# Second expert's rows asked for in front of weights, y's main part scaled first, and an early register load

## The chip, the cores and the metric

The kernel runs on one core of a Trainium2 chip. The metric is the device time of one execution in microseconds. The engines that the text names: PE is TensorE's matmul side and PEld its weight loads, DVE is VectorE, ACT is ScalarE, POOL is GpSimd, SP is SyncE, whose queue issues nearly all plain transfers. A name with a q behind it (PEq, POOLq) is the engine's sequencer.

## The reference

Sliding-window attention feeds a gated product layer, and its result goes to a mixture of eight experts with one expert per token. The last part is the one that matters here:

```python
logits = x @ w_gate
expert_idx = np.argmax(logits, axis=1)
...
gate_w = probs[np.arange(N), expert_idx]
...            # disp[e, pos] = x[i], at most `capacity` rows for each expert
h = np.maximum(np.einsum('ecd,edf->ecf', disp, w1), 0.0)
y = np.einsum('ecf,efd->ecd', h, w2)
for i in range(N):
    if keep[i]:
        out[i] = gate_w[i] * y[expert_idx[i], pos[i]]
```

There are 1152 tokens, 8 experts, d_model 512 and d_ff 1024, all in float32.

## The kernel before

Attention and the gated product layer come first. Each 128 of the resulting rows are then scattered by their expert to a table in DRAM, `disp`, with the gate weight and the token's number in two extra columns (`scatter`, L522). The largest count of tokens of any expert goes to `mxi` (L805), and 36 matmuls without use (`warm1`) follow on PE.

The expert stage goes over the experts e = 0 to 8 and over eight steps f of each (`layer1(e, f)` and, one expert behind, `layer2(e - 1, f)`). The code writes the order of the work on every engine by hand, so each engine's queue runs in the order in which the calls stand.

- `load_rows(ep, e)` (L547) reads the first 192 rows of expert e from `disp` into the tile `xr`, in two transfers of 128 and 64 rows on SP's queue.
- `x_tr(e)` (L558) transposes them on PE into two PSUM tiles `xt`; ACT (L71) and DVE (L72) split each into a high and a low part, `xs`. For expert e + 1 this is called at f = 5 of expert e.
- `layer1` (L575, L576) is four pairs of matmuls over `xs` and the weights `he`, `le`; `relu` (L583 ACT, L584 DVE, L586 ACT, L587 DVE, L590 POOL) makes `hs` of it.
- `layer2` (L604, L605 for the 64 tail rows; L607 to L609 for the 128 main rows) gathers the expert's result over its eight steps in two PSUM tiles of tag `y`, of which there are three banks. The main tile of each expert takes the bank that the main tile of the expert before had.
- `conv_e` splits the next piece of expert weights `st_e` into `he` (ACT, L71) and `le` (DVE, L72), and asks for a further piece on SP's queue (L113). With expert 0 it is called at f = 3 and f = 5 only, later at every f. The pieces have eight buffers in all, and SP waits at a piece whose buffer is not free yet, with all that is behind it in its queue.
- `y_tail` (L618 ACT, L619 DVE) scales the tail by the gate weight; `y_main` (L623 ACT) scales the main part; `y_out` (L627 POOL) scatters each to the output.

With expert 0, layer2 has no work yet, so a step is layer1 alone. Behind the expert stage the count in `mxi` is loaded to a register of each engine (L845), and a branch skips a part that is needed only if an expert has over 192 tokens.

Of the kernel before, what the change touches and what calls it, by code (L numbers as in the profile page):

```python
# [8 lines left out]
F32 = mybir.dt.float32  # L9
# [5 lines left out]
AF = mybir.ActivationFunctionType  # L15
# [3 lines left out]
P = 128  # L19
# [9 lines left out]
def block_kernel(ctx: ExitStack, tc: tile.TileContext, qT, kT, v, w1, w2, w3T, wo, wg, e1, e2, out):  # L29
    nc = tc.nc  # L30
    B, H, D, S = qT.shape
    DM = H * D
    NT = B * S
    DF = wo.shape[0] * P
    E = wg.shape[1]
# [22 lines left out]
    def slot(name, shape, dtype=F32R):  # L58
        t = big.tile([P, SLOT], dtype, tag="u", name=name)
        n = 1  # L60
        for d in shape:
            n *= d
        if len(shape) == 1:
            return t[:, :n]
        return t[:, :n].rearrange("p (a b) -> p a b", b=shape[1])
# [4 lines left out]
    def split(t, hi, lo, eng):  # L70
        nc.scalar.copy(out=hi, in_=t)  # L71
        eng.tensor_tensor(out=lo, in0=t, in1=hi.bitcast(F32), op=ALU.subtract)  # L72
# [469 lines left out]
    xr = {}  # L542

    def load_rows(ep, e):
        x = ep.tile([P, 2, RW], F32, tag="xr", name=f"xr{e}", bufs=4)
        for i, r, n in rows:
            nc.sync.dma_start(out=x[:n, i, :], in_=disp[e * CAP + r : e * CAP + r + n, :])  # L547
        xr[e] = x
# [3 lines left out]
    def x_tr(e):  # L552
        x = xr[e]
        tvs = [banks.tile([P, 512], F32, tag="t", name=f"xt{e}_{half}", bufs=2)[:, : 2 * N0].rearrange("p (a s) -> p a s", a=2) for half in range(2)]

        for i, r, n in rows:
            for dt in range(KD):
                nc.tensor.transpose(tvs[dt // 2][:, dt % 2, r : r + n], x[:n, i, dt * P : (dt + 1) * P], ident[:n, :n])  # L558
        for half, tv in enumerate(tvs):
            xt = slot(f"xs{e}_{half}", (2, 2 * N0))  # L560
            split(tv, xt[:, :, :N0], xt[:, :, N0:], nc.vector)
            xt_[e, 2 * half], xt_[e, 2 * half + 1] = xt[:, 0, :], xt[:, 1, :]
# [3 lines left out]
    def layer1(e, f):  # L566
        if f % 2 == 0:
            hs_[e, f // 2] = slot(f"hs{e}_{f // 2}", (2, 2 * N0 + NB))

        hp_ = banks.tile([P, 512], F32, tag="y" if e == 0 and f % 2 else "h", name=f"h{e}_{f}")  # L570
        hi, lo = (w.rearrange("p (k f) -> p k f", k=KD) for w in es[e, 0, f // 2])
        fs = slice(f % 2 * P, f % 2 * P + P)
        for kt in range(KD):
            xs = xt_[e, kt]
            nc.tensor.matmul(hp_[:, : 2 * N0], hi[:, kt, fs], xs, start=(kt == 0), stop=False)  # L575
            nc.tensor.matmul(hp_[:, N0 : 2 * N0], lo[:, kt, fs], xs[:, :N0], start=False, stop=(kt == KD - 1))  # L576
        live["h", e, f] = hp_

    def relu(ep, e, f, between=lambda: None):
        hp_ = live.pop(("h", e, f))  # L580
        h = hs_[e, f // 2][:, f % 2, :]
        cr = ep.tile([P, N0], F32, tag="cr", name=f"cr{e}_{f}", bufs=3)
        nc.scalar.copy(out=cr, in_=hp_[:, N0 : 2 * N0])  # L583
        nc.vector.tensor_tensor(out=hp_[:, :N0], in0=hp_[:, :N0], in1=cr, op=ALU.add)  # L584
        between()
        nc.scalar.activation(out=h[:, :N0], in_=hp_[:, :N0], func=AF.Relu)  # L586
        nc.vector.scalar_tensor_tensor(out=h[:, N0 : 2 * N0], in0=hp_[:, :N0], scalar=0.0, in1=h[:, :N0].bitcast(F32),  # L587
                                       op0=ALU.max, op1=ALU.subtract)

        nc.gpsimd.tensor_copy(h[:, 2 * N0 :], h[:, P:N0])  # L590

    yp_ = {}

    def layer2(e, kt, parts=(1, 0)):
        hi, lo = (w[:, kt % 2 * DM : kt % 2 * DM + DM] for w in es[e, 1, kt // 2])
        h = hs_[e, kt // 2][:, kt % 2, :]
        first, last = kt == 0, kt == EF // P - 1
        for tail in parts:
            if first:
                yp_[e, tail] = banks.tile([P, DM], F32, tag="y", name=f"y{tail}_{e}")  # L600
            yp = yp_[e, tail]
            if tail:
                ht = h[:, N0 + P :]
                nc.tensor.matmul(yp, ht, hi, start=first, stop=False)  # L604
                nc.tensor.matmul(yp, ht, lo, start=False, stop=last)  # L605
            else:
                nc.tensor.matmul(yp, h[:, :P], hi, start=first, stop=False)  # L607
                nc.tensor.matmul(yp, h[:, :P], lo, start=False, stop=False)  # L608
                nc.tensor.matmul(yp, h[:, N0 : N0 + P], hi, start=False, stop=last)  # L609

    ys_ = {}

    def y_tail(ep, e):
        w = xr[e][:NB, 1, DM : DM + 1]
        yb = yp_.pop((e, 1))
        y = ep.tile([P, 2, DM], F32, tag="y", name=f"y{e}")
        ys = ep.tile([P, DM], F32, tag="ys", name=f"ys{e}")
        nc.scalar.activation(out=ys[:NB], in_=yb[NB : 2 * NB], func=AF.Copy, scale=w)  # L618
        nc.vector.scalar_tensor_tensor(out=y[:NB, 1, :], in0=yb[:NB], scalar=w, in1=ys[:NB], op0=ALU.mult, op1=ALU.add)  # L619
        ys_[e] = y  # L620

    def y_main(e):
        nc.scalar.activation(out=ys_[e][:, 0, :], in_=yp_.pop((e, 0)), func=AF.Copy, scale=xr[e][:, 0, DM : DM + 1])  # L623

    def y_out(e, i):
        _, r, n = rows[i]
        put = nc.gpsimd.indirect_dma_start(  # L627
            out=out, out_offset=bass.IndirectOffsetOnAxis(ap=xr[e][:n, i, DM + 1 : DM + 2].bitcast(U32), axis=0),
            in_=ys_[e][:n, i, :], in_offset=None, bounds_check=NT - 1, oob_is_err=False)

        tc.declare_no_dep(put.ins, group="y_out", reason="rows of different tokens")
        tc.add_to_no_dep_group("y_out", put.ins)
# [129 lines left out]
    for i, u in enumerate(ab1):  # L762
# [3 lines left out]
        if i == 2:  # L766
            nc.sync.dma_start(out=disp[0 : E * CAP, :].rearrange("(p r) c -> p r c", p=P),
                              in_=zrow.unsqueeze(1).to_broadcast([P, E * CAP // P, RW]))
    for at in sorted(jobs):
        for job in jobs[at]:  # L770
            job()
    nc.sync.dma_start(out=out.rearrange("(p r) c -> p r c", p=P),
                      in_=zrow[:, :DM].unsqueeze(1).to_broadcast([P, NT // P, DM]))
# [29 lines left out]
    mxi = const.tile([P, 1], I32, name="mxi")  # L803
# [3 lines left out]
    cv_.close()  # L807
    front.close()


    ep = work.enter_context(tc.tile_pool(name="exp", bufs=2))
    banks = work.enter_context(tc.tile_pool(name="banks", bufs=3, space=bass.MemoryType.PSUM))
    deeper.append(ep)
    load_rows(ep, 0)
    x_tr(0)
    for _ in range(STAGES):
        stage_next()
    NF = EF // P
    for e in range(E + 1):
        for f in range(NF):  # L820
            if e < E:
                layer1(e, f)
                relu(ep, e, f, conv_e if e or f in (3, 5) else lambda: None)
                if f == 1 and e + 1 < E:
                    load_rows(ep, e + 1)
            if 0 < e < E:
                layer2(e - 1, f)
            if f == NF - 3 and e + 1 < E:
                x_tr(e + 1)
        if e == E:  # L830
            for part in (1, 0):
                for f in range(NF):
                    layer2(e - 1, f, (part,))
                if part:
                    y_tail(ep, e - 1)
                    y_out(e - 1, 1)
        elif e:
            y_tail(ep, e - 1)
            y_out(e - 1, 1)
        if e:  # L840
            y_main(e - 1)
            y_out(e - 1, 0)
    work.close()

    fullest = nc.values_load(mxi[0:1, 0:1], min_val=0, max_val=NT)  # L845
    with (tc.If(fullest > N0), tc.tile_pool(name="over", bufs=2) as op,
          tc.tile_pool(name="overp", bufs=2, space=bass.MemoryType.PSUM) as opp):
        for e in range(E):
# [6 lines left out]
            for r in range(N0, CAP, P):  # L855
# [16 lines left out]
                for f in range(EF // P):  # L872
                    nc.tensor.matmul(yp[:n], ht[:, f, :n], w2s[:, f, :], start=(f == 0), stop=(f == EF // P - 1))
                y = op.tile([P, DM], F32, tag="y", name=f"oy{e}_{r}")
                nc.vector.tensor_scalar_mul(y[:n], yp[:n], x[:n, DM : DM + 1])
                nc.gpsimd.indirect_dma_start(
                    out=out, out_offset=bass.IndirectOffsetOnAxis(ap=x[:n, DM + 1 : DM + 2].bitcast(U32), axis=0),
                    in_=y[:n], in_offset=None, bounds_check=NT - 1, oob_is_err=False)
# [45 lines left out]
```

## Time and profile before

| What | us |
|---|---|
| median of 3 runs | 486.1 (484.58 to 486.83) |
| the profiled execution, its own time | 483.7 |
| its span, from the first to the last instruction | 482.0 |
| PE busy | 458.3 |
| DVE busy | 322.7 |
| ACT busy | 261.6 |
| POOL busy | 143.0 |

The profiled execution lasts 1.7 us longer than its span. Busy times of an engine that others wait for say little on their own; where PE is not busy, the question is which wait ended last there.

### The profile page before, as it was taken

The numbers are of one execution on the slowest core, as the hardware profiler recorded it, in microseconds if no ns is written. First come the engines' busy times: TensorE is split into PE (matmuls) and PEld (weight loads), VectorE is DVE, ScalarE is ACT, GpSimd is POOL, SyncE is SP. The second block draws the span as 40 slices with busy tenths as digits, with TensorE's granted clock in tenths as the row PEclk, the third lists the DMA queues.
The fourth block names the chain that finished last, engine by engine and source line by source line (L and its number), as shares of the span: only waits on it lengthen the run. The fifth ranks groups of instructions, "written<-read, shape, count | busy, mean of one in ns | idle before, by whom it ended". The sixth has DMA issues, their size and how long they took to land.

```text
span 482.0 us, 9290 instructions
## 1 busy us (share of the span) xinstructions
PE 458.3 (95%) x3344; PEld 406.4 (84%) x3351; DVE 322.7 (67%) x863; ACT 261.6 (54%) x653; POOL 143.0 (30%) x151
## 2 busy tenths in 40 slices
PE   7999899999999999999999999949999999999993
PEld 3667587888999999999999998649898888888882
DVE  5788789688341645978847775246878777787740
ACT  4676667567231455344435552236767677676750
POOL 2113132213010232443402212013455454554531
PEclk9999899999999999999999999979999999999998
DMA  8655453222097233864504443354786887868001
GB/s 288 181 170 187 132 175 118 88 89 86 3 296 187 88 131 114 299 204 153 173 1 133 132 131 110 121 207 136 247 280 192 288 246 233 270 196 285 29 1 52
DMA packets 30769, 77.77 MB, mean 161 GB/s; under 512 B 3582, under 2 KB 9214, under 8 KB 30720
## 3 DMA queue, kind: packets, MB, share of 16 engines
q1 hardware_dynamic: 28976, 72.41, 48.3%
q0 software_dynamic: 1744, 4.73, 2.6%
q8 instruction: 28, 0.46, 0.4%
q14 instruction: 21, 0.17, 0.1%
HBM read 65.30 MB, written 12.61 MB: 162 GB/s over the span
## 4 chain that ended last, share of the span: by engine, by line
PE 74%; DVE 13%; ACT 4%; issue 4%; DMA 3%; SPq 1%; POOL 1%; POOLq 0%; DVEq 0%; ACTq 0%
PE h L575 10%; PE ab L373 7%; PE ab L375 6%; PE ab L374 6%; PE h L576 4%; PE x L469 4%; PE x L470 4%; PE x L471 4%; DVE t_w L140 4%; PE s L232 3%; PE t L300 3%; PE y L607 3%; PE warm L81 3%; PE oa L320 2%; PE y L608 2%
## 5 line engine op out<-in xcount | busy, mean ns | idle before, releaser
L72 DVE TENSOR_TENSOR le<-st_e,he 128x1024 fp32r<-128x1024 f32 x64 | 78.4, 1226 | 32.6 <-ACT he L71 25.9
L590 POOL CAST hs<-hs 128x64 fp32r<-128x64 f32 x64 | 56.1, 878 | 87.8 <-ACT hs L586 86.5
L575 PE MATMUL h<-xs,he 128*128 128x384 f32 x256 | 78.5, 364 | 1.1 <-DVE xs L72 1.1
L373 PE MATMUL ab<-x,wh 128*128 128x288 f32 x256 | 79.4, 310 | 0.0
L374 PE MATMUL ab<-x,wh 128*128 128x288 f32 x256 | 75.4, 295 | 0.0
L375 PE MATMUL ab<-x,wl 128*128 128x288 f32 x256 | 75.4, 294 | 0.0
L71 ACT CAST he<-st_e 128x1024 fp32r<-128x1024 f32 x64 | 67.3, 1052 | 0.0
L576 PE MATMUL h<-xs,le 128*128 128x192 f32 x256 | 64.9, 254 | 0.0
L575 PEld LDWEIGHTS h<-xs,he 128*128 128x128 f32 x256 | 49.1, 192 | 3.9 <-DVE xs L72 1.2
L373 PEld LDWEIGHTS ab<-x,wh 128*128 128x128 f32 x256 | 48.1, 188 | 4.9 <-issue 2.2
L576 PEld LDWEIGHTS h<-xs,le 128*128 128x128 f32 x256 | 49.7, 194 | 1.9
L374 PEld LDWEIGHTS ab<-x,wh 128*128 128x128 f32 x256 | 48.1, 188 | 0.0
L375 PEld LDWEIGHTS ab<-x,wl 128*128 128x128 f32 x256 | 48.0, 188 | 0.0
L383 DVE TENSOR_TENSOR g<-ab,asb 128x288 f32<-128x288 f32 x32 | 14.5, 455 | 46.1 <-PE ab L375 44.8
L258 ACT ACTIVATE p<-p,stat 128x256 f32<-128x256 f32 (+2 forms) x80 | 37.3, 470 | 13.1 <-DVE stat L247 13.0
L583 ACT COPY cr<-h 128x192 f32<-128x192 f32 x64 | 20.4, 318 | 43.4 <-PE h L576 41.4
L469 PE MATMUL x<-wph,gh 128*128 128x260 f32 x144 | 41.4, 287 | 0.0
L470 PE MATMUL x<-wpl,gh 128*128 128x260 f32 x144 | 40.6, 282 | 0.0
L471 PE MATMUL x<-wph,gl 128*128 128x260 f32 x144 | 40.6, 282 | 0.0
L378 ACT COPY asb<-ab 128x288 f32<-128x288 f32 x32 | 12.7, 397 | 47.7 <-PE ab L375 47.7
L435 PE MATMUL wp<-woh,w3h 128*128 128x260 f32 x128 | 36.3, 283 | 0.4 <-DVE wpl L72 0.4
L437 PE MATMUL wp<-woh,w3l 128*128 128x260 f32 x128 | 36.2, 283 | 0.0
(138 smaller groups left out, 1078.4 us busy)
## 6 DMA issues: line engine op xcount, KB each, us to landing
st_e<-e SPq DMA_DIRECT2D x64, 512.0 KB, 4.3
st_w<-w SPq DMA_DIRECT2D x16, 512.0 KB, 4.4
st_w<-w3T SPq DMA_DIRECT2D x16, 512.0 KB, 3.9
disp<-zrow SPq DMA_DIRECT2D x1, 4626.0 KB, 21.4
st_wo<-wo SPq DMA_DIRECT2D x8, 512.0 KB, 3.6
qk<-qT SPq DMA_DIRECT2D x8, 288.0 KB, 4.9
qk<-kT SPq DMA_DIRECT2D x8, 288.0 KB, 5.2
y<-zrow SPq DMA_DIRECT2D x1, 2304.0 KB, 10.9
```

The source lines that it names most:

```text
L71: nc.scalar.copy(out=hi, in_=t)
L72: eng.tensor_tensor(out=lo, in0=t, in1=hi.bitcast(F32), op=ALU.subtract)
L258: nc.scalar.activation(out=p[:M, j, :W], in_=p[:M, j, :W], func=AF.Exp, scale=-1.0, bias=st[:M, c : c + 1], accum_out=st[:M, 4 + c : 5 + c])
L373: nc.tensor.matmul(a[:, :NCH], hi[:, fs], xh[:, n], start=first, stop=False)
L374: nc.tensor.matmul(a[:, :NCH], hi[:, fs], xl[:, n], start=False, stop=False)
L375: nc.tensor.matmul(a[:, :NCH], lo[:, fs], xh[:, n], start=False, stop=last)
L469: nc.tensor.matmul(pa[:, :HG], gh[:, kt, :], th, start=(kt == 0), stop=False)
L470: nc.tensor.matmul(pa[:, :HG], gh[:, kt, :], tl, start=False, stop=False)
L471: nc.tensor.matmul(pa[:, :HG], gl[:, kt, :], th, start=False, stop=(kt == KF - 1))
L575: nc.tensor.matmul(hp_[:, : 2 * N0], hi[:, kt, fs], xs, start=(kt == 0), stop=False)
L576: nc.tensor.matmul(hp_[:, N0 : 2 * N0], lo[:, kt, fs], xs[:, :N0], start=False, stop=(kt == KD - 1))
L590: nc.gpsimd.tensor_copy(h[:, 2 * N0 :], h[:, P:N0])
```

## The change

The rows of expert 1 are asked for right behind those of expert 0, in front of four pieces of expert weights, where they stood behind these. After each expert ACT scales the main part of y ahead of the tail, where it scaled the tail first. And the largest count is loaded to the engines' registers ahead of the expert stage, where it was loaded behind it.

```diff
+    def y_tile(ep, e):
+        if e not in ys_:
+            ys_[e] = ep.tile([P, 2, DM], F32, tag="y", name=f"y{e}")
+        return ys_[e]
+
     def y_tail(ep, e):
         w = xr[e][:NB, 1, DM : DM + 1]
         yb = yp_.pop((e, 1))
-        y = ep.tile([P, 2, DM], F32, tag="y", name=f"y{e}")
+        y = y_tile(ep, e)
...
-    def y_main(e):
-        nc.scalar.activation(out=ys_[e][:, 0, :], in_=yp_.pop((e, 0)), func=AF.Copy, scale=xr[e][:, 0, DM : DM + 1])
+    def y_main(ep, e):
+        nc.scalar.activation(out=y_tile(ep, e)[:, 0, :], in_=yp_.pop((e, 0)), func=AF.Copy, scale=xr[e][:, 0, DM : DM + 1])
...
+    fullest = nc.values_load(mxi[0:1, 0:1], min_val=0, max_val=NT)
...
     load_rows(ep, 0)
+    load_rows(ep, 1)
     x_tr(0)
     for _ in range(STAGES):
         stage_next()
...
-                if f == 1 and e + 1 < E:
+                if f == 1 and e and e + 1 < E:
                     load_rows(ep, e + 1)
...
-        elif e:
+        if e:
+            y_main(ep, e - 1)
+        if 0 < e < E:
             y_tail(ep, e - 1)
             y_out(e - 1, 1)
         if e:
-            y_main(e - 1)
             y_out(e - 1, 0)
     work.close()
-    fullest = nc.values_load(mxi[0:1, 0:1], min_val=0, max_val=NT)
```

SP's queue at the start of the expert stage, before the change; `xr_4006` are the rows of expert 0, `xr_4064` those of expert 1, and `st_e` are pieces of weights:

```order
L845 TENSOR_LOAD mxi
L845 ISA x2
L547 DMA xr_4006<-disp 128x514
L547 DMA xr_4006<-disp 64x514
L113 DMA st_e_0_3_4025<-e 128x1024
L113 DMA st_e_1_0_4027<-e 128x1024
L113 DMA st_e_0_0_4029<-e 128x1024
L113 DMA st_e_1_1_4031<-e 128x1024
L547 DMA xr_4064<-disp 128x514
L547 DMA xr_4064<-disp 64x514
L113 DMA st_e_0_1_4095<-e 128x1024
```

The same place with the change, where `xr_4020` and `xr_4023` are the rows of experts 0 and 1:

```order
L814 TENSOR_LOAD mxi
L814 ISA x2
L547 DMA xr_4020<-disp 128x514
L547 DMA xr_4020<-disp 64x514
L547 DMA xr_4023<-disp 128x514
L547 DMA xr_4023<-disp 64x514
L113 DMA st_e_0_3_4042<-e 128x1024
L113 DMA st_e_1_0_4044<-e 128x1024
L113 DMA st_e_0_0_4046<-e 128x1024
L113 DMA st_e_1_1_4048<-e 128x1024
L113 DMA st_e_0_1_4109<-e 128x1024
```

Expert 1's two transfers moved past four pieces of weights; SP's own register load stood here already.

ACT at the end of an expert's eight steps, before the change (the last `hs`, the tail's scale, the main part's scale, then the first step of the next expert):

```order
L586 ACTIVATE hs_3_4368<-h_7_4395 128x192
L618 ACTIVATE ys_4422<-y_0_4210,xr_4006 64x512
L623 ACTIVATE y_4421<-y_0_4213,xr_4006 128x512
L583 COPY cr_0_4442<-h_0_4433 128x192
L71 CAST he_1_3_4447<-st_e_1_3_4229 128x1024
```

The same place with the change:

```order
L586 ACTIVATE hs_3_4382<-h_7_4409 128x192
L627 ACTIVATE y_4435<-y_0_4227,xr_4020 128x512
L623 ACTIVATE ys_4437<-y_0_4224,xr_4020 64x512
L583 COPY cr_0_4456<-h_0_4447 128x192
L71 CAST he_1_3_4461<-st_e_1_3_4243 128x1024
```

The two scales changed places; nothing else on ACT moved there.

PE between the matmuls without use and the transposes of expert 0's rows, with the change:

```order
L81 LDWEIGHTS hot
L81 MATMUL warm_3956<-hot 128x512
L814 TENSOR_LOAD mxi
L558 MATMUL xt_0_4026<-ident,xr_4020 128x128 x2
L558 MATMUL xt_1_4027<-ident,xr_4020 128x128 x2
L558 MATMUL xt_0_4026<-ident,xr_4020 128x64 x2
```

The register load is new in this place; before the change it stood behind PE's last matmul. On DVE, ACT and POOL it moved in the same way, to the place ahead of their first work for expert 0.

## Rows read from the trace of the kernel before

**Rows 1.** The page, PE's busy tenths in 40 slices of the span.

```profile
PE   7999899999999999999999999949999999999993
```

**Rows 2.** Stretches: length, busy PE, PEld, DVE, ACT, POOL, granted clock, DMA share, GB/s.

```profile
306.00:315.20 9.20, 8.05 (x56) 7.59 (x56) 4.37 (x10) 4.51 (x12) 1.29 (x4) 1.00 0.29 102
315.20:321.60 6.40, 0.04 (x1) 0.00 (x1) 3.05 (x7) 1.72 (x4) 1.77 (x3) 0.90 0.77 259
321.60:327.10 5.50, 5.47 (x22) 5.05 (x23) 1.57 (x4) 1.51 (x4) 0.15 (x1) 0.50 0.39 151
...
386.60:406.60 20.00, 19.71 (x114) 17.33 (x114) 15.75 (x27) 14.18 (x29) 9.84 (x10) 1.00 0.80 251
```

**Rows 3.** Timeline of SP's queue: start, length, queue, line, operation, tiles, count.

```profile
302.22 0.89 SPq L547 DMA_DIRECT2D xr<-disp  x2
...
315.61 0.80 SPq L113 DMA_DIRECT2D st_e<-e  x2
316.46 0.96 SPq L547 DMA_DIRECT2D xr<-disp  x2
```

**Rows 4.** Timeline of PE around the transposes; in brackets its idle time and what ended it.

```profile
308.17 0.45 PE L575 MATMUL h<-xs,he 128*128 128x384 f32 x1 [1.08 <-DVE xs L72]
...
321.63 1.71 PE L558 MATMUL xt<-ident,xr 128*128 128x128 f32 x8 [6.38 <-DMA xr<-disp]
...
327.44 0.36 PE L575 MATMUL h<-xs,he 128*128 128x384 f32 x1
...
341.17 0.99 PE L558 MATMUL xt<-ident,xr 128*128 128x128 f32 x8
342.09 0.45 PE L575 MATMUL h<-xs,he 128*128 128x384 f32 x1
```

**Rows 5.** Timeline of ACT and DVE, 317 to 325 us.

```profile
317.53 0.34 ACT L586 ACTIVATE hs<-h 128x192 fp32r<-128x192 f32 x1
318.81 0.35 DVE L587 SCALAR_TENSOR_TENSOR hs<-h,hs 128x192 fp32r<-128x192 f32 x1
...
323.16 0.86 ACT L71 CAST xs<-xt 128x384 fp32r<-128x384 f32 x2 [5.29 <-PE xt L558]
...
323.67 1.02 DVE L72 TENSOR_TENSOR xs<-xt,xs 128x384 fp32r<-128x384 f32 x2 [4.51 <-ACT xs L71]
```

**Rows 6.** Waits by pairs of lines: total us, times, longest.

```profile
PEld y L607 <- ACT y L623: 4.4, 6, 0.7
```

**Rows 7.** Timeline of PE, PEld and ACT where the loop goes from e = 3 to 4.

```profile
385.48 0.41 PE L604 MATMUL y<-he,hs 128*128 128x512 f32 x1
...
386.66 0.34 PE L575 MATMUL h<-xs,he 128*128 128x384 f32 x1
...
387.26 0.69 ACT L618 ACTIVATE ys<-y,xr 64x512 f32<-64x512 f32 x1
...
387.77 0.41 PE L604 MATMUL y<-he,hs 128*128 128x512 f32 x1
...
387.97 0.69 ACT L623 ACTIVATE y<-y,xr 128x512 f32<-128x512 f32 x1
...
388.71 0.19 PEld L607 LDWEIGHTS y<-he,hs 128*128 128x128 f32 x1 [0.72 <-ACT y L623]
...
389.51 0.34 PE L575 MATMUL h<-xs,he 128*128 128x384 f32 x1
```

**Rows 8.** The register loads of L845 (ns, start) on PE and POOL; PE's last matmul.

```profile
L845 PEldq TENSOR_LOAD <-mxi x1: 685/685/685, 470.4 to 470.4; - x1
...
L845 POOLq TENSOR_LOAD <-mxi x1: 500/500/500, 475.3 to 475.3; - x1
...
474.19 0.39 PE L609 MATMUL y<-he,hs 128*128 128x512 f32 x1
```

**Rows 9.** DMA issues of 300 to 306 us: count, size, us from issue to landing.

```profile
xr<-disp SPq DMA_DIRECT2D x1, 257.0 KB, 2.7
xr<-disp SPq DMA_DIRECT2D x1, 128.5 KB, 3.4
```

More of the change, by code (lines that the diff above doesn't have):

```diff
@@ L619, in y_tail @@
         nc.vector.scalar_tensor_tensor(out=y[:NB, 1, :], in0=yb[:NB], scalar=w, in1=ys[:NB], op0=ALU.mult, op1=ALU.add)
-        ys_[e] = y
-    def y_main(e):
-        nc.scalar.activation(out=ys_[e][:, 0, :], in_=yp_.pop((e, 0)), func=AF.Copy, scale=xr[e][:, 0, DM : DM + 1])
+    def y_main(ep, e):
+        nc.scalar.activation(out=y_tile(ep, e)[:, 0, :], in_=yp_.pop((e, 0)), func=AF.Copy, scale=xr[e][:, 0, DM : DM + 1])
     def y_out(e, i):
```

## The prediction

> **What bounds the kernel now.** I read the page's slices first: PE is busy for nine tenths and more nearly throughout, but one slice in the later half drops to 4 [rows 1]. The stretches show what that slice is: from 315.2 to 321.6 us PE does nothing, and in the 5.5 us behind it the granted clock is 0.50, the lower of PE's two levels (1.2 of 2.4 GHz) [rows 2]. PE's timeline names the wait. The transposes of expert 1's rows start at 321.63 after 6.38 us of idle time that the transfer of `xr` ended [rows 4]. SP's queue says why the rows came late: expert 0's rows were asked for at 302.22, but expert 1's at 316.46 only, behind two pieces of weights that went out at 315.61 when a buffer came free [rows 3]. So the queue was the cause, and not the transfer's length.
>
> The second place is smaller and comes six times: the weight load of L607, the first main matmul of an expert's layer 2, waits for ACT's L623, 4.4 us in total and at most 0.7 [rows 6]. That matmul writes into the bank that L623 still reads, and ACT takes L618 before L623 [rows 7].
>
> **The rows of expert 1.** With the change they are asked for right behind expert 0's, whose two issues take 0.89 us: at about 303.1 us [rows 3]. Expert 0's landed 2.7 and 3.4 us after issue [rows 9]; even with twice 3.4 us, expert 1's are there by 310, and PE wants them at 321.63 - 6.38 = 315.25. So the wait for the rows goes, all of it.
>
> What is late next? The transposes' results go through ACT and DVE, and these run behind PE at that point: with expert 0 a step of PE is layer 1 alone. Their own work there doesn't depend on the rows, so its times hold. ACT is free at 317.53 + 0.34 = 317.87, and its two casts (0.86) end at 318.73. DVE is free at 318.81 + 0.35 = 319.16, and its two subtractions (1.02) end at 319.67 and 320.18 [rows 5]. PE in the meantime has little to do. An unhindered set of transposes takes 342.09 - 341.17 = 0.92 us to the next matmul [rows 4]; a layer-1 step of four pairs takes 387.77 - 386.66 = 1.11 us at full clock [rows 7], and steps 6 and 7 of expert 0 are left. PE would be ready for expert 1 at 315.25 + 0.92 + 2.22 = 318.39 and starts at 319.67, when the first half of `xs` is there: a new wait of 1.28 us. The second half (320.18) is there before two pairs (0.56) are through, at 320.23. Before, this first matmul of expert 1 stood at 327.44 [rows 4]. The gain is 327.44 - 319.67 = 7.77 us, and it contains the slow clock of 321.6 to 327.1, since no long wait precedes. If the new wait were nothing, it would be 327.44 - 318.39 = 9.05.
>
> The four pieces of weights that stand behind now go out about 0.9 us later, at most; two of them waited for a buffer until 315.61 anyway [rows 3]. None is split before expert 1's steps. Expert 0's own rows now share the transfer engines with expert 1's, and with weights somewhat later. The price lies between 0 and 2.7 us (their landing doubled); I take 0, since before the change pieces of 512 KB stood in the same place.
>
> **The main part first.** Where no wait is, a step's five layer-2 matmuls take 386.66 - 385.48 = 1.18 us; at the change of experts they take 389.51 - 387.77 = 1.74 [rows 7]. That is 0.56 us, and by the six waits [rows 6] 3.36 us. With the change ACT starts the main scale where the tail's stood, at 387.26, and ends it 0.69 later at 387.95. The weight load followed 0.05 us behind the end of L623 before (387.97 + 0.69 = 388.66, then 388.71), so now it can go at 388.00 and, at 0.19 us, is through at 388.19; five matmuls in 1.18 us are 0.236 each, so that L607 as the third, unhindered, starts at 387.77 + 0.47 = 388.24 [rows 7]. It fits by 0.05 us. The tail's scale and DVE's L619 behind it come 0.7 and at most 0.7 us later; nothing of the next steps reads what they write, since the tails use the two other banks in turn. Behind them in ACT's queue the copies of the next step start no later than before, as the two scales are equally long. On DVE the shift meets slack: 15.75 us busy of 20.00 in such a stretch, ACT 14.18 [rows 2]. DMA is at 0.80 there and has 3 per cent less time per expert, which leaves it under 0.83. The bounds are 0 and 3.36; I take 3.36, nearest to the rows.
>
> **The register loads.** On PE the load takes 0.685 us. Before, it ran at 470.4, though the last matmul ahead of it in the program started at 474.19: PE's sequencer is some 3.8 us ahead of its matmuls, and the load doesn't wait for them to end [rows 8]. Now it stands behind 36 matmuls without use, which cover it, and ahead of transposes that wait for rows anyway. DVE, ACT and POOL wait for the same rows. Cost 0; without the cover 0.7. At the end POOL's 0.50 us could come off if the branch were on the end's path: between 0 and 0.5, and I take 0, as the last scatter has to land in any case.
>
> **The sum.** 7.77 + 3.36 = 11.13 us. The profiled execution took 483.7 us, which makes 472.6. The median of the runs shown, 486.1, is 2.4 above it, and so I forecast 486.1 - 11.1 = **475.0 us**.
>
> **The rivals.** *The clock falls in the new wait.* PE then waits 1.28 us behind two steps of expert 0, and if its clock falls to the lower level for as long as it did before (5.5 us at 0.50, rows 2), half of that is lost: 2.75 us, so 477.8. Against it: 1.08 us of idle time ahead of expert 0's first matmul left the clock at 1.00 over that stretch [rows 2, 4]. The Trainium skill, in "TensorE: Matmul & The Clock Gate", section "Part 1: The HAM clock gate (the "warmup" mystery)", says that idleness puts the clock back to half and that activity has to earn it again; by that rule every new wait of PE is suspect, and the trace agrees for the 6.38 us, not for the 1.08.
>
> *The new wait is shorter*, because ACT and DVE come through sooner once no transfer crowds them: up to 9.05 in place of 7.77, so 473.7. Nothing in the rows speaks for it.
>
> *The order of the scales gives nothing*, because L607 then waits for something that ends as late, the tail's DVE part for one: 475.0 + 3.4 = 478.4. Against it: L607 went on 0.05 us behind L623, and the margin of 0.05 is thin but there.
>
> *The rows' early request does nothing*, because PE meets another wait of the same length at 315: only 3.4 us would come off, 482.7. For it speaks only that ACT and DVE are late there, and by 1.28 us, not 6.
>
> *Slower.* The place is expert 1. Short waits at its start keep the clock at the lower level, not for 5.5 us but throughout. Each microsecond of full-speed work then costs a second one, so from 11.1 us of such work on the gain is used up; over one expert (20.0 us, rows 2) it is 486.1 - 11.1 + 20.0 = 495. Against it: the clock came back within 5.5 us last time.
>
> **How the numbers follow.** Chances: the forecast 0.62, the clock's fall 0.12, the shorter wait 0.08, no gain from the scales 0.10, no gain from the rows 0.04, slower 0.04. From no change a measurement of this kernel tells about 0.5 per cent, 2.4 us, so faster means below 483.7. The first four cases lie there, and so would the fifth by a microsecond, which I count mostly as no change: faster 0.93, same 0.03, slower 0.04. The range goes from 473.7 to 478.4 by the cases and by the runs' own spread, about 1.2 us below and less above: 472.5 to 479.0.
>
> **What would show it.** Right: SP asks for both experts' rows within 2 us; the transposes of expert 1 follow on layer 1 without a wait for a transfer; a wait of about 1.3 us for DVE's L72 ahead of expert 1's first matmul; a granted clock of 1.00 from 306 on; the wait of L607 for ACT gone in all six places, and some 19.3 us per expert. Wrong: the clock at 0.50 behind the transposes, a wait of L607 for DVE, transposes of expert 0 later than 306.1, or pieces of weights that ACT's L71 waits for in expert 1.

## The result and the profile after

The changed kernel takes 472.1 us (median of 4 runs, 471.56 to 475.0), against 485.34 for the kernel before in the same comparison (4 runs, 484.32 to 486.83). The ratio is 0.976, with a 95% interval of 0.9725 to 0.9796: faster, as forecast. The time forecast was 475.0. The profiled execution took 471.56 us with a span of 469.7, which is 12.3 under the 482.0 of before.

The page of the changed kernel: its span, and PE's busy tenths in 40 slices, as in [rows 1].

```profile
span 469.7 us, 9304 instructions
...
PE   7999899999999999999999999999999999999993
```

The slice with a 4 is gone. The stretches of the changed kernel (length, busy PE, PEld, DVE, ACT, POOL, granted clock, DMA share, GB/s) answer to [rows 2]:

```profile
306.00:315.20 9.20, 8.12 (x58) 7.83 (x58) 5.30 (x12) 4.58 (x13) 1.77 (x4) 1.00 0.29 98
315.20:318.40 3.20, 2.30 (x16) 2.07 (x15) 2.37 (x5) 2.63 (x7) 1.30 (x2) 1.00 0.87 293
318.40:319.80 1.40, 1.13 (x7) 1.13 (x8) 1.00 (x4) 0.42 (x2) 0.03 (x1) 1.00 0.68 138
...
340.00:360.00 20.00, 20.00 (x118) 17.94 (x116) 16.49 (x29) 14.88 (x30) 10.33 (x10) 1.00 0.77 256
```

Two things are to be seen. The granted clock is 1.00 in each of them, where it was 0.50 for 5.5 us before. And PE is busy for 20.00 of the 20.00 us between 340 and 360, where a like stretch had 19.71 of 20.00.

SP's queue of the changed kernel, for [rows 3]:

```profile
301.16 2.05 SPq L547 DMA_DIRECT2D xr<-disp  x4
303.26 20.81 SPq L113 DMA_DIRECT2D st_e<-e  x8
```

Both experts' rows, four transfers, go out in 2.05 us, and the pieces of weights follow. PE's timeline, for [rows 4]:

```profile
307.14 0.45 PE L575 MATMUL h<-xs,he 128*128 128x384 f32 x1 [1.08 <-DVE xs L72]
...
314.06 0.99 PE L558 MATMUL xt<-ident,xr 128*128 128x128 f32 x8
...
318.67 0.44 PE L575 MATMUL h<-xs,he 128*128 128x384 f32 x1 [1.17 <-DVE xs L72]
```

The second row is expert 1's transposes, with no wait noted behind it; the third is the first matmul of expert 1, with the new wait. ACT and DVE, for [rows 5], show why it is there:

```profile
316.51 0.34 ACT L586 ACTIVATE hs<-h 128x192 fp32r<-128x192 f32 x1
316.66 1.23 DVE L72 TENSOR_TENSOR le<-st_e,he 128x1024 fp32r<-128x1024 f32 x1 [0.53 <-ACT he L71]
316.74 0.87 ACT L71 CAST xs<-xt 128x384 fp32r<-128x384 f32 x2
...
317.80 0.35 DVE L587 SCALAR_TENSOR_TENSOR hs<-h,hs 128x192 fp32r<-128x192 f32 x1
318.07 1.01 DVE L72 TENSOR_TENSOR xs<-xt,xs 128x384 fp32r<-128x384 f32 x2
```

DVE comes to `xs` at 318.07 only, behind the low half of a piece of weights (1.23 us) and a step's `hs`; PE goes on at 318.67, when the first of the two subtractions is through.

The change of experts from e = 3 to 4, on PE and ACT, for [rows 7]:

```profile
375.62 0.41 PE L604 MATMUL y<-he,hs 128*128 128x512 f32 x1
...
376.80 0.34 PE L575 MATMUL h<-xs,he 128*128 128x384 f32 x1
...
377.26 0.70 ACT L627 ACTIVATE y<-y,xr 128x512 f32<-128x512 f32 x1
...
377.91 0.41 PE L604 MATMUL y<-he,hs 128*128 128x512 f32 x1
377.98 0.69 ACT L623 ACTIVATE ys<-y,xr 64x512 f32<-64x512 f32 x1
...
378.40 0.39 PE L607 MATMUL y<-he,hs 128*128 128x512 f32 x1
...
379.08 0.33 PE L575 MATMUL h<-xs,he 128*128 128x384 f32 x1
```

L627 is now the main scale and L623 the tail's. The five layer-2 matmuls take 379.08 - 377.91 = 1.17 us at the change of experts, as within an expert (376.80 - 375.62 = 1.18), and the waits' view has no row of L607 any more. From one expert's transposes to the next it is 371.18 - 351.82 = 19.36 us, where it was 381.04 - 361.08 = 19.96. The register load, for [rows 8], in ns:

```profile
L814 DVEq TENSOR_LOAD <-mxi x1: 541/541/541, 297.6 to 297.6; - x1
...
L814 PEldq TENSOR_LOAD <-mxi x1: 491/491/491, 300.9 to 300.9; - x1
```

PE's sequencer does it at 300.9, more than 4 us ahead of the transposes that stand behind it in the program (305.04).

For all that follows, three instants of each profile's timeline are read: the start of expert 0's transposes, the start of the first layer-2 matmul (L604 in the kernel before, expert 1's step 0), and the start of the last one. Between the first two lies the wait for the rows with its clock; between the others lie the six changes of experts. In every profile but one the span ends 7.77 us behind the last (7.91 with the gap filled).

| Kernel | transposes | first L604 | last matmul | first to second | second to third |
|---|---|---|---|---|---|
| before | 306.07 | 328.57 | 474.19 | 22.50 | 145.62 |
| changed | 305.04 | 319.89 | 461.96 | 14.85 | 142.07 |
| rows only | 305.02 | 319.87 | 465.39 | 14.85 | 145.52 |
| scales only | 305.17 | 329.04 | 471.12 | 23.87 | 142.08 |
| register only | 309.86 | 333.75 | 479.39 | 23.89 | 145.64 |
| split at step 6 | 305.36 | 319.05 | 461.12 | 13.69 | 142.07 |
| gap filled | 305.93 | 326.32 | 471.94 | 20.39 | 145.62 |
| tail twice | 306.43 | 329.97 | 479.78 | 23.54 | 149.81 |
| register in expert 3 | 304.72 | 319.59 | 461.68 | 14.87 | 142.09 |
| splits at 6 and 7 | 307.28 | 320.71 | 463.97 | 13.43 | 143.26 |

### The profile page after: what moved, and what is told of

Read it like the earlier page. It is cut to its first block, busy times and chain, and to the rows that moved or that the text cites. A ratio compares the mean times of both kernels' runs of the same rounds, so it can differ in the third digit from the quotient of the medians.

```text
span 469.7 us, 9304 instructions
## 1 busy us (share of the span) xinstructions
PE 452.2 (96%) x3351; PEld 403.8 (86%) x3351; DVE 322.7 (69%) x863; ACT 262.1 (56%) x653; POOL 142.6 (30%) x151
## 4 chain that ended last, share of the span: by engine, by line
PE 74%; DVE 15%; issue 4%; ACT 3%; DMA 2%; POOL 1%; SPq 1%; DVEq 0%; POOLq 0%; ACTq 0%
PE h L575 10%; PE ab L373 7%; PE ab L375 6%; PE ab L374 6%; PE h L576 4%; PE x L469 4%; DVE t_w L140 4%; PE x L470 4%; PE x L471 4%; PE warm L81 3%; PE t L300 3%; PE y L604 3%; PE s L232 3%; PE y L607 3%; PE y L605 3%
## 5 line engine op out<-in xcount | busy, mean ns | idle before, releaser
L575 PE MATMUL h<-xs,he 128*128 128x384 f32 x256 | 76.8, 358 | 2.3 <-DVE xs L72 2.3
L575 PEld LDWEIGHTS h<-xs,he 128*128 128x128 f32 x256 | 48.0, 188 | 5.2 <-DVE xs L72 2.6
L576 PEld LDWEIGHTS h<-xs,le 128*128 128x128 f32 x256 | 48.7, 190 | 1.9
```

## The experiments

### One part of the change at a time

Rows only, on the kernel before:

```diff
     load_rows(ep, 0)
+    load_rows(ep, 1)
     x_tr(0)
...
-                if f == 1 and e + 1 < E:
+                if f == 1 and e and e + 1 < E:
```

> Of the kernel before, with expert 1's rows asked for in front of the four pieces of weights, and nothing else. My theory, rows 7.8 us and scales 3.4 us and register load 0: 7.8 us faster than before (ratio 0.984), expert 1's transposes without a wait for a transfer, a wait of 1.2 us for DVE's L72 ahead of expert 1's first matmul, and the six waits of L607 for ACT (4.4 us) still there. A rival, that the parts need each other or that a good part of the 12.3 us between the two profiled spans comes from the register load: 5 us or less.

475.67 us (6 runs), against 484.32 for the kernel before in the same series (23 runs): ratio 0.9828 (0.9795 to 0.9862), 8.65 us. The first stretch of the table is that of the changed kernel, 14.85 us, the second that of before. Its waits (total us, times, longest) hold the old one of L607 and the new one for DVE, which stands in one row with the 1.08 us ahead of expert 0's first matmul:

```profile
PEld y L607 <- ACT y L623: 4.4, 6, 0.7
...
PE h L575 <- DVE xs L72: 2.3, 2, 1.2
```

Scales only (the lines of `y_tile`, `y_tail`, `y_main` and their calls as in the change):

```diff
-        elif e:
+        if e:
+            y_main(ep, e - 1)
+        if 0 < e < E:
             y_tail(ep, e - 1)
             y_out(e - 1, 1)
         if e:
-            y_main(e - 1)
             y_out(e - 1, 0)
```

> Of the kernel before, with the main part scaled ahead of the tail, and nothing else. My theory: 3.4 us faster (ratio 0.993), no wait of L607 for ACT in the six places, and the gap of 6.4 us ahead of expert 1's transposes as before. A rival, that the waits go only because the whole stage is shifted by the earlier rows, or that another wait takes their place: within 1 us of before.

481.0 us (12 runs), against the same 484.32: ratio 0.9934 (0.991 to 0.9958), 3.3 us. The second stretch is 142.08 us, that of the changed kernel, the first is long. No row of L607 is left in its waits, and the wait for the rows is there:

```profile
PE xt L558 <- DMA xr<-disp: 6.9, 1, 6.9
```

Register load only:

```diff
     front.close()
 
+    fullest = nc.values_load(mxi[0:1, 0:1], min_val=0, max_val=NT)
...
     work.close()
 
-    fullest = nc.values_load(mxi[0:1, 0:1], min_val=0, max_val=NT)
```

> Of the kernel before, with the register load ahead of the expert stage, and nothing else. My theory: no change (within 0.5 us), PE's load 4 us ahead of the matmuls that run then, and expert 0's transposes at the end of the matmuls without use as before. A rival, that the load was on the end's path or stands in PE's way now: 0.5 us faster or 0.7 us slower, and in the profile the end behind the last matmul, 7.8 us long before, shorter, or the transposes later.

485.27 us (12 runs), ratio 1.0009 (0.9978 to 1.004): no change that these runs can tell, though the interval still has room for one to two microseconds either way. The second stretch and the 7.77 us behind the last matmul are those of before, and expert 0's transposes follow on the matmuls without use. So the parts add up: 0.9828 times 0.9934 times 1.0009 is 0.977, and the whole change has 0.976.

### Where the 7.8 us are: the wait and the clock

Thirty matmuls without use in front of expert 1's transposes, in the kernel before. They compute nothing that is used.

```diff
+            if f == NF - 3 and e == 0:
+                w = banks.tile([P, 512], F32, tag="t", name="warm2", bufs=2)
+                for _ in range(30):
+                    nc.tensor.matmul(w, hot[:, :P], hot, start=True, stop=True)
             if f == NF - 3 and e + 1 < E:
                 x_tr(e + 1)
```

> Of the kernel before, with 30 matmuls without use (128x512, as those ahead of the expert stage) in front of expert 1's transposes, where PE otherwise waits 6.4 us for the rows. They compute nothing that is used. My theory, that of the 7.8 us some 2.7 are the clock that falls over the idle gap: the rows land as late as before, the granted clock stays at 1.00, and the time is 2.7 us under before (ratio 0.9945). A rival, that the transposes themselves or expert 1's start bring the clock down: it falls anyway, and the time is that of before.

481.58 us (9 runs), against 485.35 (20 runs): ratio 0.9909 (0.9877 to 0.9942), 3.8 us where I had forecast 2.7. The rows land as late as before, expert 1's transposes start 15.95 us behind expert 0's (15.56 before), and the clock stays up. The stretches of this kernel:

```profile
315.20:321.90 6.70, 6.35 (x30) 2.75 (x29) 2.90 (x7) 1.72 (x4) 1.62 (x3) 1.00 0.78 256
321.90:327.40 5.50, 5.50 (x37) 5.11 (x38) 2.84 (x7) 2.98 (x8) 0.47 (x2) 1.00 0.36 141
```

So the idle gap brings the clock down, and not the transposes. The first stretch of the table is 20.39 us: 2.1 less than in the profile of before, but 3.1 to 3.5 less than in the three other profiles in which the wait is left (23.54 to 23.89). The profile of "register only" shows what differs:

```profile
319.00:325.70 6.70, 0.03 (x1) 0.00 (x0) 3.03 (x7) 1.71 (x4) 1.76 (x3) 0.82 0.80 250
325.70:333.50 7.80, 7.74 (x31) 7.32 (x32) 2.43 (x6) 2.16 (x6) 0.48 (x2) 0.50 0.27 105
```

There the clock is at 0.50 for 7.8 us of matmuls, where [rows 2] have 5.5. What the wait costs varies from execution to execution, and the profile on which I forecast was the mildest of four. The difference has two parts. Expert 1's transposes started 15.56 us behind expert 0's in the profile of before and 15.87 to 16.04 in the other three, since the rows landed later there. From these transposes to the first L604 it took 6.94 us before, 7.67 to 7.99 in the other three and 4.44 with the gap filled: the slow clock cost 2.5 us in the one and 3.2 to 3.6 in the others.

### Double the wait of L607

In the kernel before, ACT's tail scale is done twice in a row, with the same result:

```diff
         nc.scalar.activation(out=ys[:NB], in_=yb[NB : 2 * NB], func=AF.Copy, scale=w)
+        nc.scalar.activation(out=ys[:NB], in_=yb[NB : 2 * NB], func=AF.Copy, scale=w)
```

> Of the kernel before, with the tail's scale on ACT (L618) done twice in a row, the second time with the same result. My theory, that L607's six waits are the place of the main scale in ACT's queue: each grows by the 0.69 us of one such scale, 4.1 us in all (ratio 1.0085), and the waits of L607 for ACT in the profile go from 4.4 to about 8.5 us. A rival, that the waits end with the matmuls of the main part or with something else that is late there: 1 us or less.

489.14 us (12 runs), against 485.35: ratio 1.0072 (1.0042 to 1.0102); the second stretch grows by 149.81 - 145.62 = 4.19 us. The waits of this kernel, in which the main scale is L624:

```profile
PEld y L607 <- ACT y L624: 8.7, 6, 1.5
```

From 4.4 to 8.7 us, by one scale of 0.69 us six times. The cause of these waits is the main scale's place in ACT's queue.

### The register load without its cover

In the changed kernel, the load in the midst of expert 3:

```diff
-    fullest = nc.values_load(mxi[0:1, 0:1], min_val=0, max_val=NT)
...
         for f in range(NF):
+            if e == 3 and f == 2:
+                fullest = nc.values_load(mxi[0:1, 0:1], min_val=0, max_val=NT)
             if e < E:
                 layer1(e, f)
```

> Of the changed kernel, with the register load not ahead of the expert stage but in the middle of expert 3 (ahead of its step 2), where every engine is at work and nothing waits for rows. My theory: PE's sequencer is ahead of its matmuls by more than the load's 0.5 to 0.7 us there too, and the other engines have idle time left, so it costs nothing: the time of the changed kernel within 0.5 us. A rival, that the load was free only under the cover of the matmuls without use: 0.5 to 1.2 us more than the changed kernel, and a gap in PE's matmuls at that place.

473.38 us (6 runs), ratio 0.9739 (0.9695 to 0.9783), which can't be told from the changed kernel's 0.976 (0.9725 to 0.9796); the second stretch is 142.09 against 142.07 us. Two engines' loads, in ns:

```profile
L827 PEldq TENSOR_LOAD <-mxi x1: 486/486/486, 358.5 to 358.5; - x1
L827 ACTq TENSOR_LOAD <-mxi x1: 464/464/464, 362.2 to 362.2; - x1
```

PE's sequencer does it 3.7 us before ACT comes to the same place. Cover or not, it costs nothing that these profiles show.

### The new wait, and a version that is faster

In the changed kernel, expert 0's second split of weights is put off by one step, behind the making of expert 1's `xs`:

```diff
-                relu(ep, e, f, conv_e if e or f in (3, 5) else lambda: None)
+                relu(ep, e, f, conv_e if e or f in (3, 6) else lambda: None)
```

> Of the changed kernel, with expert 0's second split of weights moved from step 5 to step 6, so that it stands behind the casts and subtractions that make expert 1's xs. My theory, that the new wait of 1.17 us is ACT's and DVE's late work and that this split (1.06 us on ACT, 1.23 us on DVE) is what makes it late: the wait at expert 1's first matmul falls to 0.1 us or less, and the time by 1.1 us against the changed kernel (ratio to before 0.974). A rival, that the wait moves on, since the split only comes later: the same time as the changed kernel, with a new wait of about 1 us on PE in expert 1.

470.88 us (6 runs), ratio 0.9726 (0.9689 to 0.9763). The first stretch is 13.69 us, 1.16 less than in the changed kernel; of the wait the view of waits keeps only

```profile
PEld h L575 <- DVE xs L72: 0.2, 1, 0.2
```

To compare the two on one chip, both ran again in one series.

> The changed kernel itself, timed beside the next two on the same chip. Expected: the ratio to before that was measured first, 0.976, and the wait of 1.17 us ahead of expert 1's first matmul.

> The kernel with expert 0's second split at step 6 once more, to compare it with the changed kernel on one chip. My theory: 1.2 us under the changed kernel (0.25 per cent), and from expert 0's transposes to the first layer-2 matmul 13.7 us as in its first profile, 14.85 in the changed kernel. A rival, that its first profile was a lucky one: no difference between the two.

The changed kernel: 472.31 us (6 runs, 472.01 to 473.91), ratio to before 0.9766 (0.9738 to 0.9793), the wait 1.17 us again. With the split at step 6: 471.24 us (5 runs, 471.19 to 471.7), ratio 0.9741 (0.9712 to 0.9769), and 13.69 us again. The intervals of the ratios overlap, but the runs don't, and 472.31 - 471.24 = 1.07 us is close to the 1.16 that the profiles show.

Both splits put off:

```diff
-                relu(ep, e, f, conv_e if e or f in (3, 5) else lambda: None)
+                relu(ep, e, f, conv_e if e or f in (6, 7) else lambda: None)
```

> Of the changed kernel, with both of expert 0's splits of weights behind the making of expert 1's xs, at steps 6 and 7 in place of 3 and 5. My theory: PE's wait is gone already with one of them moved, so this gives no more: the time of the kernel with the split at step 6, within 0.5 us. A rival, that a split put off is late for the matmuls of expert 1 or keeps SP from asking for weights in time: PE waits in expert 1 for ACT's L71, DVE's L72 or POOL's L590, 1 us or more.

471.89 us (5 runs, 470.89 to 473.47), ratio 0.9743 (0.9713 to 0.9772). The median is 0.65 us above that of the split at step 6, but the runs of the two overlap, so the time decides little; the profile sides with the rival. The first stretch wins another 0.26 us (13.43), the second loses 1.19 (143.26 against 142.07), and PE's timeline shows where:

```profile
334.44 1.04 PE L558 MATMUL xt<-ident,xr 128*128 128x128 f32 x8 [0.96 <-DMA xr<-disp]
```

These are the transposes of expert 2's rows, and again they wait for the rows, but not because these were asked for late. SP's queue ahead of them, and the time from issue to landing of the 128 rows:

```profile
321.25 4.13 SPq L113 DMA_DIRECT2D st_e<-e  x6
325.42 1.38 SPq L547 DMA_DIRECT2D xr<-disp  x2
...
xr<-disp SPq DMA_DIRECT2D x1, 257.0 KB, 9.0
```

The same in the second run of the split at step 6:

```profile
320.53 4.12 SPq L113 DMA_DIRECT2D st_e<-e  x4
324.70 0.98 SPq L547 DMA_DIRECT2D xr<-disp  x2
...
xr<-disp SPq DMA_DIRECT2D x1, 257.0 KB, 5.3
```

Counted from expert 0's transposes, the rows are asked for at 325.42 - 307.28 = 18.14 us with both splits put off and at 324.70 - 305.87 = 18.83 with one: earlier, if anything. But they landed 9.0 us after issue, where it was 5.3. The two late splits give buffers back late and close together, so six pieces of weights go out in the 4.13 us ahead of the rows, where it was four; from 316 to 321 us the transfer engines had stood still (DMA share 0.00, against 0.57 with one split put off). That the bunched pieces made the rows' transfer long fits these numbers, but no run tests it by itself. I had looked for the rival on ACT, DVE and POOL; it came through the transfers. By the sum of the two stretches, 155.76 us against 156.69, one split at step 6 is the best of these versions; the times alone don't tell the two apart.

## Why the prediction was right, step by step

**The wait for the rows** went, for the reason given. The profiles say 22.50 - 14.85 = 7.65 us for the first stretch; I had 7.77. Both figures stand on the one profile of before, so what their agreement bears out is the new start: 319.67 - 306.07 = 13.60 us behind expert 0's transposes by the forecast, 318.67 - 305.04 = 13.63 measured. The new wait was worked out as 1.28 us and measured 1.17, in its place and with the engine that was named. The chain behind it, ACT and DVE late by their own work, held when "split at 6" took that work away.

**The clock.** I had left the slow stretch inside the 7.77 us and taken its length from one profile. That is the term that was mis-sized: in the three other profiles with the wait the first stretch is 23.54 to 23.89 us, so there the rows are worth 8.7 to 9.0, and the medians of "rows only" say 8.65. The rival of a clock that falls in the new wait did not come about: with 1.17 us of idle time the granted clock stayed at 1.00 in that stretch, as it had with 1.08. The rule of the Trainium skill that I weighed ("TensorE: Matmul & The Clock Gate", "Part 1: The HAM clock gate (the "warmup" mystery)"), that idleness puts the clock back, agrees with the filled gap, where the clock stayed, and with the open one, where it fell. The section does not say that a wait of any length does this, so the 1.08 us, and now the 1.17, are not against it as I had put it.

**The main part first** gave 145.62 - 142.07 = 3.55 us, with 3.36 forecast: 0.59 for each of six. The margin of 0.05 us sufficed: L604 to the next L575 takes 1.17 us at the change of experts. The rival that L607 would wait for DVE instead has no row.

**The register load** cost nothing that a profile shows and gave nothing back at the end: behind the last matmul 7.77 us are left in both kernels.

**The sum.** Forecast 11.13 us from the profile; the two stretches give 7.65 + 3.55 = 11.20. The two spans differ by 12.3, and the other 1.03 us (306.07 - 305.04) lie ahead of expert 0's transposes. Of the change only the register load stands there, and it is not the reason: without it, "rows only" and "scales only" start these transposes at 305.02 and 305.17. The ratio that I forecast was 475.0 / 486.1 = 0.977, and the range, taken the same way, 0.972 to 0.985; the measured 0.976 lies in it. The time itself, 472.1, still lies 0.4 us under the range's lower end of 472.5. Two things moved it: the median of before, on which the forecast stood, was 486.1 by three runs and 485.34, 484.32, 485.35 and 483.51 in the comparisons since; and the wait with its slow clock cost more in the three other profiles than in the one I read. The two kernels timed together once more differ by 483.51 - 472.31 = 11.2 us, where the first comparison, of four runs each, has 13.2. The range had allowed for the runs' own spread by 1.2 us, and for a dearer wait in the kernel before not at all.

## What to carry to other kernels

In a queue that runs in order, a transfer is as late as the wait of whatever stands ahead of it. Small transfers that are needed soon belong in front of large ones that wait for a buffer; the row to look for first is the issue's time, and then the time from issue to landing, which was what went wrong with both splits put off. When a wait is taken away, work out when each engine behind it will be free by its own work: here it gave the next wait to a tenth of a microsecond, and the place from which the next 1.1 us came. And where two results wait on one engine, the one whose bank is wanted first goes first.

## What the runs showed that I had not expected

The opening of the kernel, the same in all these kernels but for the register load at its end, varies by more than the second part of the change is worth: expert 0's transposes start between 304.72 us ("register in expert 3") and 309.86 ("register only") in the ten profiles of the table. In the slowest of them the granted clock was 0.89 over the first 30 us, in the changed kernel 1.00; from 30 to 60 us it was 0.94 in the kernel before, in the changed one 1.00. Most of the spread of a kernel's runs (482.81 to 487.85 for the kernel before in one series) may be of this kind; no run here tests it. Behind expert 0's transposes the profiles agree to about a tenth of a microsecond wherever PE has no long wait, so that a part of the program is better judged by the distance between two of its own instructions than by the span.
